# A grouped 1x1 convolution over 512x512 pixels: other runs of rows, other ends of the stores

## The chip, the cores and the metric

The kernel runs on one core of a Trainium2 chip. The metric is the device time of one execution in microseconds (us); the figure for a kernel is the median of its runs. Engines are called by the names that the profile gives them: PE is the matmul engine (PEld its weight loads), DVE the vector engine, ACT the scalar engine, POOL the GpSimd engine and SP the engine that here only issues transfers. SPq, ACTq and POOLq are their sequencers. The core's 16 DMA engines move data between the large memory (HBM) and the on-chip memory (SBUF), whose 128 rows are called partitions.

## The reference, cut to what matters

```python
H = W = 512; G = 4; Cg = 48; C = 192; k = 1
# x: (1, 512, 512, 192) bfloat16, w: (1, 1, 4, 48, 48) bfloat16
xg = x.reshape(1, 512, 512, 4, 48)
out = einsum('bhwgc,gcd->bhwgd', xg, w[0, 0])
return out.reshape(1, 512, 512, 192)
```

For each of 262,144 pixels, four groups of 48 channels are each multiplied by a 48x48 matrix. 100.7 MB are read and as much is written.

## The kernel before

**Columns and fields.** A pixel has 192 values of 2 bytes, 384 bytes. The image is laid out as fields one behind the other. In a full field each of the 128 partitions holds a run of consecutive pixels; its length in pixels is the field's number of columns. A column is thus one pixel in each partition, 49,152 bytes. `plan_fields` (L84) makes, from `FRONT` (L46): a full field of 560 columns, a partial field of 48, full fields of 32 and 880, a partial one of 48, full ones of 32 and 456, which is 2056 columns. In a partial field (`PARTIAL`, L41) only 120 of the 128 partitions hold pixels: all but 16 to 19 and 48 to 51. It moves in five blocks of rows, two of 16 rows through SP and ACT, and three of 44, 12 and 32 rows through POOL. The numbers of a block are its queue, first row, rows, the outer size of its DRAM pattern (4, 4, 11, 3 and 8, so 4 rows of each part belong together), and the columns that it has less. `UNEVEN` (L45) takes 16 columns from the first block of the second partial field, so that the rest of the image divides by 4 x 128 pixels. PE and ACT work on all 128 partitions of such a field; the unused ones are not stored.

**Rings.** The input ring `ring` holds 240 columns, three slots of 80. The output ring `oring` holds 280. `plan_pieces` (L102) cuts fields into loads: 8, 24 and 48 columns first (`HEAD`), then 80 each, and a partial field in one piece. A partial field's 48 columns and the 32 of the full field behind it fill one slot together, a mixed slot. A column's place in the ring is its number modulo 240 (L72 and L256). `plan_stores` (L116) cuts fields into stores at the ring's places 72, 140, 212 and 280 (`OGRID`), at most 40 columns long in the last 240 and with ends at the last 68, 44, 24 and 8 columns (`LAST_PARTS`).

**Engines.** SP (L312) issues the loads in order; each waits until PE has transposed the columns whose place it takes (`freed`, L264). PE works on groups of 4 columns, two groups to a pair: 12 transposes through the identity into PSUM (L350), then, one pair behind, 12 matmuls (L370) with a block matrix that L332 built from the weights. PE waits for a load's semaphore at the first group of a slot; a mixed slot is released by POOL, which waits for all its parts (L299, L300). PE's pairs 9 to 248 run in a loop of 8 rounds of 30 pairs, since a round of 60 groups returns to the same place in the ring. DVE copies the transposes to SBUF (L409). ACT copies each group's result into the output ring (L446) and issues a store once the group after its last has been computed (L427); before it writes to a place it waits for the store that left from there (`landed`, L420). POOL issues its blocks of the partial fields (L296, L307) and, ahead of the blocks of 44 and 12 rows, a small filler transfer (L286).

**Queues.** Loads that SP issues go through queue q1, stores of ACT through q10, POOL's transfers through q0.

Of the kernel before, what the change touches and what calls it, by code (L numbers as in the profile page):

```python
# [1 line left out]

# [22 lines left out]
BIG = 80  # L25
SLOTS = 3
RCOLS = SLOTS * BIG
OGRID = (72, 140, 212, 280)
OCOLS = OGRID[-1]
HEAD = (8, 24, 48)  # L30
LATE_COLS = 240
LATE_PART = 40
LAST_PARTS = (24, 20, 16, 8)
# [5 lines left out]
FULL = (("sync", 0, 128, 128, 0),)  # L39

PARTIAL = (  # L41
    ("sync", 0, 16, 4, 0), ("sync", 32, 16, 4, 0),
    ("pool", 52, 44, 11, 0), ("pool", 20, 12, 3, 0), ("pool", 96, 32, 8, 0),
)
UNEVEN = (("sync", 0, 16, 4, 16), *PARTIAL[1:])  # L45
FRONT = ((6, ((48, PARTIAL), (32, FULL))), (11, ((48, UNEVEN), (32, FULL))))  # L46

FILL_ROWS = 5
FILL_BEFORE = (2, 3)


class Field:


    def __init__(self, cols, blocks, g0, pix):
        self.cols, self.g0, self.g1 = cols, g0, g0 + cols // 4
        self.full = blocks is FULL
        self.blocks = []
        for (queue, r0, rows, outer, less) in blocks:
            self.blocks.append((queue, r0, rows, outer, pix, cols - less))  # L60
            pix += rows * (cols - less)
        self.pix_end = pix
        assert cols % 4 == 0


class Piece:

    def __init__(self, i, field, c0, size):
        self.i, self.field = i, field
        self.c0, self.c1, self.size = c0, c0 + size, size  # L70
        self.g0, self.g1 = field.g0 + self.c0 // 4, field.g0 + self.c1 // 4
        self.at = 4 * self.g0 % RCOLS  # L72
        self.full, self.blocks = field.full, field.blocks
        assert size % 4 == 0 and self.at + size <= RCOLS

# [7 lines left out]

def plan_fields(npix):  # L84

    parts, head = [], sum(HEAD)
    for slots, special in FRONT:
        parts += [(head + BIG * slots, FULL), *special]
        head = 0
    cols = npix - sum((n - b[4]) * b[2] for n, blocks in parts for b in blocks)  # L90
    if cols < 128 * BIG:
        parts, cols = [], npix
    assert cols % 512 == 0
    fields, g, pix = [], 0, 0
    for n, blocks in [*parts, (cols // 128, FULL)]:
        fields.append(Field(n, blocks, g, pix))
        g, pix = fields[-1].g1, fields[-1].pix_end
    assert pix == npix
    return fields


def plan_pieces(fields):  # L102
    pieces = []
    for f in fields:
        first = [f.cols]
        if f.full:
            first = list(HEAD) if not f.g0 and sum(HEAD) <= f.cols else []
        c = 0
        while c < f.cols:
            n = first.pop(0) if first else min(BIG, f.cols - c)  # L110
            pieces.append(Piece(len(pieces), f, c, n))
            c += n
    return pieces


def plan_stores(fields):  # L116
    total = 4 * fields[-1].g1
    stores, at = [], 0
    for f in fields:
        c = 0  # L120
        if not f.full and at + f.cols > OCOLS:
            at = 0
        ends = []
        if f is fields[-1] and f.cols > LATE_COLS:
            ends = [f.cols - sum(LAST_PARTS[i:]) for i in range(len(LAST_PARTS))]
        while c < f.cols:
            if f.full:
                end = min([g for g in OGRID if g > at + 24] or [OCOLS]) - at + c
                if f.cols < BIG:
                    end = min(OCOLS - at + c, f.cols)  # L130
                if ends and c >= f.cols - LATE_COLS:
                    end = min(OCOLS - at, LATE_PART) + c
                end = min([end, f.cols] + [e for e in ends if e > c])
            else:
                end = f.cols
            stores.append(Store(f, c, end, at))
            c, at = end, (at + end - c) % OCOLS
    return stores


class Unit:


    def __init__(self, pieces):
        self.pieces, self.g0, self.g1 = pieces, pieces[0].g0, pieces[-1].g1
        self.slot = pieces[0].at // BIG
        self.regular = pieces[0].at % BIG == 0 and 4 * (self.g1 - self.g0) == BIG


def plan_units(pieces):  # L150
    units, rest = [], list(pieces)
    while rest:
        n = 1
        if rest[0].g0 and rest[0].at % BIG == 0:
            while n < len(rest) and rest[n].at % BIG:
                n += 1
        units.append(Unit(rest[:n]))
        rest = rest[n:]
    return units
# [19 lines left out]
def bass_standalone__grouped__vision_kernel(nc, x, w, out):  # L179
# [3 lines left out]
    assert npix % 512 == 0, "the pixel count must be a multiple of 512"  # L183

    fields = plan_fields(npix)
    pieces = plan_pieces(fields)
    stores = plan_stores(fields)
    units = plan_units(pieces)
    unit_of = {g: u for u in units for g in range(u.g0, u.g1)}
    store_of = {g: s for s in stores for g in range(s.g0, s.g1)}  # L190
# [12 lines left out]
    def transfers(ap, tile, part, queues):  # L203
        f, c0, c1, at = part.field, part.c0, part.c1, part.at
        for n, (queue, r0, rows, outer, pix, cols) in enumerate(f.blocks):
            if queue not in queues:
                continue
            px = ap[pix:pix + rows * cols, :]
            if f.full:
                view = px.rearrange("(p i) n -> p (i n)", p=rows)[:, c0 * C:c1 * C]  # L210
            else:
                assert (c0, c1) == (0, f.cols)
                view = px.rearrange("(c a i) n -> a c (i n)", a=outer, c=rows // outer)
            yield n, view, tile[r0:r0 + rows, at * C:(at + (c1 - c0 if f.full else cols)) * C]
# [12 lines left out]
    with ExitStack() as es:  # L227
# [25 lines left out]
        fill_sem = [sem(f"fill{k}") for k in range(4 * len(mixed))]  # L253

        def columns(g):
            at = 4 * g % RCOLS  # L256
            return ring[:, at * C:(at + 4) * C]

        def out_columns(g):
# [9 lines left out]
        def _(gp):  # L269
# [12 lines left out]
            def filler():  # L282
                k = len(used)
                src = xf[0:2 * FILL_ROWS, 0:4].rearrange("(t p) n -> p t n", t=2)
                dst = fill[:, 8 * k:8 * k + 8].rearrange("p (t n) -> p t n", t=2)
                gp.dma_start(dst, src).then_inc(fill_sem[k], 16)  # L286
                used.append(k)

            for nth, u in enumerate(mixed):
                part = [p for p in u.pieces if not p.full]  # L290
                for p in part:
                    gp.wait_ge(t_done, freed(p))
                    for n, dram, sbuf in transfers(xf, ring, p, ("pool",)):
                        if n in FILL_BEFORE:
                            filler()
# [6 lines left out]
                for i, s in enumerate(stores):  # L302
                    if any(s.field is p.field for p in part):
                        for n, dram, sbuf in transfers(of, oring, s, ("pool",)):
                            if n in FILL_BEFORE:
                                filler()
# [174 lines left out]
```

## Time and profile before

| what | us |
|---|---|
| median of 9 runs | 477.94 (477.2 to 479.64) |
| profiled execution | 477.95 |
| its span, first to last instruction | 476.2 |
| ACT: 514 copies of a group, 801 ns each | 387.4 |
| DVE: 257 copies of a pair, 958 ns each | 246.2 |
| PE busy | 431.5 |
| 22 loads of 3840 KB, median from issue to landing | 27.0 |
| 11 stores of 3456 KB, the same | 41.2 |
| 10 stores of 3264 KB, the same | 41.4 |
| first store issued by ACT at | 26.3 |
| last load issued by SP at | 409.3 |

The span is the profiled execution's time from its first to its last instruction; 1.75 us of its time lie around it. Busy times of different engines overlap, and a transfer's time from issue to landing includes the time that it stands in a queue. The page's two rows in 40 digits, DMA and GB/s, give the state of the DMA engines over the span.

### The profile page before, as it was taken

Reading aid. Unit: us, or ns where it says so; the run is one execution under the profiler, and the core shown is the slowest. Engines: PE = TensorE matmul, PEld = TensorE weight load, DVE = VectorE, ACT = ScalarE, POOL = GpSimd, SP = SyncE. Lnnn points to the kernel's source line nnn. Section 1 sums busy time; section 2 is a strip of 40 time slices with the busy share of each in tenths; the row PEclk is TensorE's granted clock in tenths of the full one; section 3 lists DMA queues with packets and bytes.
Section 4 is the critical chain, followed back from the end, with each engine's and each line's share of the span. In section 5 each row is a group of like instructions: output and inputs, shape, how many; then the busy total and the mean of one; then the engine's idle time right before and its main releaser. Section 6 shows DMA issues by size and latency. Waiting matters only on the chain.

```text
span 476.2 us, 13580 instructions
## 1 busy us (share of the span) xinstructions
PE 431.5 (91%) x6178; PEld 390.3 (82%) x6178; DVE 246.9 (52%) x258; ACT 388.7 (82%) x515; POOL 12.5 (3%) x28
## 2 busy tenths in 40 slices
PE   4999999999698999999997996999978998997993
PEld 4988889888697898888896896898877987886882
DVE  2555555555354555555553553555545555552551
ACT  2898899988587998998895885999868997976884
POOL 1000000200002000000000000200002000000000
PEclk9999999999899999999998997999989999998997
DMA  8999999999999999999999999999999999999997
GB/s 327 434 399 429 431 431 430 423 428 437 437 430 427 431 424 435 436 437 422 427 433 437 437 430 422 435 421 439 431 432 428 432 427 426 424 437 433 422 414 294
DMA packets 10674, 201.57 MB, mean 423 GB/s; under 512 B 2112, under 2 KB 2112, under 8 KB 2752
## 3 DMA queue, kind: packets, MB, share of 16 engines
q1 hardware_dynamic: 4320, 97.44, 48.0%
q10 hardware_dynamic: 5120, 97.42, 47.8%
q0 software_dynamic: 1216, 6.49, 3.3%
q8 instruction: 9, 0.15, 0.1%
q14 instruction: 9, 0.07, 0.0%
HBM read 100.68 MB, written 100.66 MB: 423 GB/s over the span
## 4 chain that ended last, share of the span: by engine, by line
PE 48%; DMA 39%; ACT 8%; issue 1%; ACTq 1%; another core or an unknown queue 1%; SPq 0%; POOLq 0%
DMA out_dram<-oring 30%; PE o_ps L370 28%; PE xT_ps L350 20%; DMA ring<-in_x_dram 9%; ACT oring L446 8%; ACTq L427 1%; SPq L320 0%; SPq L313 0%; ACTq L420 0%; POOLq L300 0%; POOLq L299 0%; ACTq L429 0%
## 5 line engine op out<-in xcount | busy, mean ns | idle before, releaser
L446 ACT CAST oring<-o_ps 128x768 bf16<-128x768 f32 x514 | 387.4, 801 | 80.2 <-PE o_ps L370 55.3
L409 DVE COPY xT_sb<-xT_ps 128x1536 bf16<-128x1536 bf16 x257 | 246.2, 958 | 216.7 <-PE xT_ps L350 216.7
L370 PE MATMUL o_ps<-wt,xT_sb 128*128 128x144 bf16 (+1 forms) x3084 | 290.0, 237 | 27.2 <-ACT oring L446 21.5
L370 PEld LDWEIGHTS o_ps<-wt,xT_sb 128*128 128x128 bf16 x3084 | 213.3, 99 | 65.6 <-ACT oring L446 56.2
L350 PE MATMUL xT_ps<-ident,ring 128*128 128x128 bf16 x3084 | 222.2, 223 | 7.0 <-POOLq L300 3.6
L350 PEld LDWEIGHTS xT_ps<-ident,ring 128*128 128x128 bf16 x3084 | 190.2, 100 | 9.7 <-POOLq L300 3.8
L286 POOL DMA_DIRECT2D fill<-in_x_dram x8 | 4.6, 575 | 350.6 <-PE xT_ps L350 235.8
L296 POOL DMA_DIRECT2D ring<-in_x_dram x6 | 3.4, 562 | 0.0
L307 POOL DMA_DIRECT2D out_dram<-oring x6 | 3.3, 558 | 0.0
L332 PE MATMUL o_ps<-w_sb,esel 48*128 48x48 bf16 x10 | 0.6, 210 | 2.7 <-DMA w_sb<-in_w_dram 2.7
L332 PEld LDWEIGHTS o_ps<-w_sb,esel 48*128 48x128 bf16 x10 | 0.5, 113 | 2.7 <-POOL esel L273 2.7
L402 DVE CAST wt<-o_ps 128x480 bf16<-128x480 f32 x1 | 0.7, 658 | 3.3 <-PE o_ps L332 3.3
L446 ACT ACT_TABLE_LOAD x1 | 1.3, 1283 | 0.8 <-PEq L466 0.8
L273 POOL TENSOR_SCALAR_AFFINE_SELECT esel<-esel 48x272 bf16<-48x272 bf16 x1 | 0.4, 404 | 0.0
L270 POOL MEMSET esel<- 48x272 bf16 x1 | 0.3, 318 | 0.3 <-POOLq L466 0.3
L277 POOL TENSOR_SCALAR_AFFINE_SELECT ident<-ident 128x128 bf16<-128x128 bf16 x1 | 0.3, 284 | 0.0
L271 POOL MEMSET ident<- 128x128 bf16 x1 | 0.2, 198 | 0.0
L466 POOL MEMSET const-float32-0.0<- 128x1 f32 x1 | 0.1, 99 | 0.3 <-issue 0.3
L466 POOL MEMSET const-bfloat16-1.0<- 128x1 bf16 x1 | 0.1, 103 | 0.0
L466 POOL MEMSET const-uint8-127<- 128x1 uint8 x1 | 0.1, 103 | 0.0
L466 POOL MEMSET const-float32-1.0<- 128x1 f32 x1 | 0.1, 99 | 0.0
## 6 DMA issues: line engine op xcount, KB each, us to landing
ring<-in_x_dram SPq DMA_DIRECT2D x22, 3840.0 KB, 27.0
out_dram<-oring ACTq DMA_DIRECT2D x11, 3456.0 KB, 41.2
out_dram<-oring ACTq DMA_DIRECT2D x10, 3264.0 KB, 41.4
out_dram<-oring ACTq DMA_DIRECT2D x3, 1920.0 KB, 19.5
out_dram<-oring ACTq DMA_DIRECT2D x1, 3840.0 KB, 47.4
ring<-in_x_dram SPq DMA_DIRECT2D x2, 1536.0 KB, 31.3
out_dram<-oring ACTq DMA_DIRECT2D x2, 1536.0 KB, 43.3
out_dram<-oring ACTq DMA_DIRECT2D x1, 2880.0 KB, 39.0
```

The lines of the kernel that those rows point to most:

```text
L273: gp.affine_select(out=esel[:], in_=esel[:], pattern=[[-1, ECOLS]], compare_op=AluOpType.is_equal, fill=0.0, base=ESHIFT, channel_multipli ...
L286: gp.dma_start(dst, src).then_inc(fill_sem[k], 16)
L296: gp.dma_start(sbuf, dram).then_inc(ld_sem[ld_key[p.i, n]], 16)
L307: gp.dma_start(dram, sbuf).then_inc(st_sem[i][n], 16)
L332: last = pe.matmul(o_ps[:, NOB - 1, col:col + CG], lhsT=esel[:, s0:s0 + 128], rhs=w_sb[:, g, :], start=True, stop=True, skip_group_check=True)
L350: last = pe.transpose(xT_ps[:, g % NXP, j * 128:(j + 1) * 128], xg[:, j * 128:(j + 1) * 128], ident[:])
L370: last = pe.matmul(o_ps[:, v % NOB, c0_:c1_], lhsT=xs[:, j * 128:(j + 1) * 128], rhs=wt[:, WOFF[tc]:WOFF[tc] + (c1_ - c0_)], start=(tc == ...
L402: dve.tensor_copy(wt[:], o_ps[:, NOB - 1, 0:WCOLS]).then_inc(wc_sem, 1)
L409: dve.tensor_copy(xT_sb[pair % NXS][:, 0:n * 2 * UC].rearrange("p (g c) -> p g c", g=n), xT_ps[:, b0:b0 + n, 0:2 * UC]).then_inc(e_done[pa ...
L427: act.dma_start(dram, sbuf).then_inc(st_sem[i][n], 16)
L446: act.copy(out_columns(g).rearrange("p (u c) -> p u c", u=2), o_ps[:, v % NOB:v % NOB + 2, 0:UC]).then_inc(fa_done[g % (2 * NTOK)] if g < ...
L466: nc = _bacc.Bacc("TRN2", target_bir_lowering=False, num_devices=1)
```

## The change

`OGRID` becomes (92, 188, 280): a store ends at about each third of the output ring instead of each quarter. The first field's stores end after 8, 32 and 92 columns (`FIRST_STORES`). The head is 88 columns (8, 24, 56) instead of 80, and the place of a column in the input ring becomes its number less 88, modulo 240, so that the head ends at the ring's end and the slots begin with column 88. The partial fields have 44 columns, and the first 36 of the full field behind each fill the slot; those 36 are no field of their own any more but the first piece of a run of 916 or 484. `UNEVEN` takes 11 columns from the first block and 12 from the block of 12 rows.

The loads are then 8, 24, 56, 6 of 80, 44, 36, 11 of 80, 44, 36, 5 of 80 and 48. The stores are 8, 24, 60, 96, 92, 92, 96, 92 and 8 columns, the partial 44, then 40, 96, 92, 92, 96, 92, 92, 96, 92, 92 and 36, the partial 44, and 108, 92, 96, 40, 40, 12, 28, 24, 20, 16 and 8. PE's loop covers pairs 10 to 249.

```diff
-OGRID = (72, 140, 212, 280)
+OGRID = (92, 188, 280)
-HEAD = (8, 24, 48)
+HEAD = (8, 24, 56)
+FIRST_STORES = (8, 24, 60)
-UNEVEN = (("sync", 0, 16, 4, 16), *PARTIAL[1:])
-FRONT = ((6, ((48, PARTIAL), (32, FULL))), (11, ((48, UNEVEN), (32, FULL))))
+UNEVEN = (("sync", 0, 16, 4, 11), *PARTIAL[1:3], ("pool", 20, 12, 3, 12), PARTIAL[4])
+FRONT = ((6, 44, PARTIAL), (11, 44, UNEVEN))
+def ring_at(g):
+    return (4 * g - sum(HEAD)) % RCOLS
...
-        self.at = 4 * self.g0 % RCOLS
+        self.at = ring_at(self.g0)
...
-    parts, head = [], sum(HEAD)
-    for slots, special in FRONT:
-        parts += [(head + BIG * slots, FULL), *special]
-        head = 0
+    parts, lead = [], sum(HEAD)
+    for slots, cols, blocks in FRONT:
+        parts += [(lead + BIG * slots, FULL), (cols, blocks)]
+        lead = BIG - cols
...
-            n = first.pop(0) if first else min(BIG, f.cols - c)
+            n = first.pop(0) if first else min(BIG - ring_at(f.g0 + c // 4) % BIG, f.cols - c)
...
-        ends = []
+        ends = list(accumulate(FIRST_STORES)) if not f.g0 else []
...
-                if ends and c >= f.cols - LATE_COLS:
+                if f is fields[-1] and c >= f.cols - LATE_COLS:
...
-        self.regular = pieces[0].at % BIG == 0 and 4 * (self.g1 - self.g0) == BIG
+        self.regular = self.g0 > 0 and pieces[0].at % BIG == 0 and 4 * (self.g1 - self.g0) == BIG
...
-        if rest[0].g0 and rest[0].at % BIG == 0:
+        if 4 * rest[0].g0 >= sum(HEAD) and rest[0].at % BIG == 0:
...
-            at = 4 * g % RCOLS
+            at = ring_at(g)
```

## The prediction

> **What bounds the kernel now.** I read the page's list of busy times first, then its DMA queues, then the waits, and last the timeline around two places: where compute stops for a load, and the end.
>
> ```profile
> span 476.2 us, 13580 instructions
> PE 431.5 (91%) x6178; PEld 390.3 (82%) x6178; DVE 246.9 (52%) x258; ACT 388.7 (82%) x515; POOL 12.5 (3%) x28
> ...
> DMA  8999999999999999999999999999999999999997
> ...
> q1 hardware_dynamic: 4320, 97.44, 48.0%
> q10 hardware_dynamic: 5120, 97.42, 47.8%
> q0 software_dynamic: 1216, 6.49, 3.3%
> ```
>
> The 16 DMA engines are busy from the second slice to the last but one, and the three queues of data add up to 99.1% of their span. PE at 91% is no bound: ACT's copies go at one per 0.828 us where nothing stops them (column 80 at 27.46 us, column 160 at 44.33), so 514 of them need 425 us. The bytes are the floor: 201.57 MB at the plateau of 432 GB/s (the trace's packets of 30,720 bytes take 1,138 ns on each of 16 engines) is 466.6 us.
>
> ```profile
> DVE xT_sb L409 <- PE xT_ps L350: 216.7, 257, 6.3
> ...
> ACT oring L446 <- PE o_ps L370: 55.3, 135, 8.3
> ...
> ACT oring L446 <- DMA out_dram<-oring: 18.2, 8, 4.7
> ...
> PE xT_ps L350 <- POOLq L300: 3.6, 1, 3.6
> PE xT_ps L350 <- DMA ring<-in_x_dram: 3.4, 2, 1.9
> ```
>
> So compute waits for the DMA almost only on the store side: ACT stops 8 times until an old store has left the output ring. PE waits for a load once after the head, in the first mixed slot (pieces of 48 and 32 columns), and ACT then stands 4.75 us:
>
> ```profile
> 130.28 1.60 ACT L446 CAST oring<-o_ps 128x768 bf16<-128x768 f32 x2 [4.75 <-PE o_ps L370]
> ...
> 431.06 1.50 ACT L446 CAST oring<-o_ps 128x768 bf16<-128x768 f32 x2 [4.71 <-DMA out_dram<-oring]
> ...
> 469.73 0.50 ACTq L427 DMA_DIRECT2D out_dram<-oring  x1
> ```
>
> The last stop ends at 431.06; from there ACT makes 44 copies in 38.6 us without a stop, issues the last store at 469.73, and the trace has that store's engines landing between 472.56 and 475.72. Both chains thus end together, and neither has much to spare.
>
> **What the skill says.** "DMA: Bandwidth & Descriptors", section "Queues, rings and completion order": each DMA engine takes the queues that have work in turn, a packet at a time. The DMA view between 200 and 250 us agrees:
>
> ```profile
> q1 hardware_dynamic: 418, 11.37, 52.7%
> q10 hardware_dynamic: 422, 10.15, 47.3%
> ```
>
> As many packets of loads as of stores, and so bytes in the ratio of their sizes (80 columns against 68 or 72). The same page, "The descriptor swizzle", puts rows 16 to 19 and 48 to 51 of a 128-row transfer on one engine, the fifth; these are the rows that the 120-row pieces leave out. The trace agrees: after the first such piece one engine lands its part of the stores 7.2 us before the middle one, and loses 3.7% of time from there (lead 7.2 us at 194, 3.4 at 300). And "Where 436 GB/s comes from" gives a ceiling of 435 GB/s, beside 432 measured: no size of packet can bring more than 0.7%.
>
> **The change, part by part.** I count in columns: 128 rows of 384 bytes, 0.1138 us at 432 GB/s. There are 2056 to load and 2056 to store, in both kernels (560+48+32+880+48+32+456 and 568+44+916+44+484), 467.9 us of DMA. By the packet records the sum of columns moved at time t is (t - c) / 0.1138 with c = 4.2 us at 84, 4.7 at 264 and 5.6 at 444.
>
> *Number of transfers.* Loads stay 30 pieces; stores fall from 37 to 33. A packet of 3,072 bytes takes 121 ns and one of 30,720 takes 1,138, so each has about 8 ns of its own; 4 stores of 8 rows per engine less is 32 x 8 ns = 0.26 us gained. Issues on ACT (0.34 us) and SP lie beside DMA work: 0.
>
> *Head and first stores.* The first store is issued near 13 us, not 26.34. The loads fill the DMA until then, so nothing is gained: 0. Where the stores begin now, the DMA share falls to 0.51 between 30 and 31 us, about 1 us lost over the dip; whether smaller first stores shrink it no row shows: -0.9 to 0, I take 0. The third piece lands some 0.9 us later (8 columns more), before its first transpose at 14.78 us: 0. The ring now starts at column 152, so the second 80-column piece waits for the first pair of transposes (6.2 us) with 88+80 columns, 19 us of DMA, queued: 0.
>
> *Thirds.* Store packets become 35,328 or 36,864 bytes beside loads of 30,720, so the turn about now favours stores by 53.5 to 46.5, where it favoured loads by 53 to 47. The store queue drains as fast as ACT fills it, and ACT's 18.2 us of waits for stores go. What is late next are the loads: they lose 0.74 columns per us against ACT (4.09 against 4.83).
>
> *Mixed slots.* On the first four engines a 44-column piece takes 8 packets and the 36-column piece behind it another 8, each in turn with a store packet of 1.31 to 1.36 us. PE waits for the last of them. The sum of columns gives its time. For the kernel before, with 640 loaded and 437 stored on those engines, 1077 x 0.1138 + 4.5 + 0.8 for the landing = 127.9, and the trace has 127.85. After, at most 648 loaded and 560 stored (more isn't issued yet): 137.4 + 5.3 = 142.8, so ACT resumes column 568 at 145.2 (2.4 us later, as before) instead of 128.8: idle 16.4 us, not 4.75. In the second slot at most 1608 + 1492: 352.7 + 6.0 = 358.8, and column 1528 is copied at 361.2 (before: near 347, though column 1600 at 366.6 after ACT's own waits). POOL issues the same 20 transfers; its last load of each slot landed at 124.56 and 336.63 before, 38 and 33 us after its issue, and is not the last to land now: 0. The bound from below is the kernel before: a wait of 4 us; I take the upper one, since the stores are ready in time.
>
> *Does the DMA run dry behind these waits?* Just ahead of the next load's issue at column 728, 888 columns of loads and 652 of stores are out, 1540, and 1520 are moved: 2.3 us in hand. At column 1688: 3420 against 3412, 0.9 us. Nothing is lost, barely.
>
> *End.* From 361.2, 352 columns at 0.2069 us bring ACT to column 1880 at 434.0; the same 38.6 us as before end it at 472.6, against 469.7; the fastest landing seen after the last issue was 2.8 us, so 475.5 at the latest from this chain. The DMA chain: 88 columns of stores are still queued when ACT reaches 1990, so the starved windows of the end (0.92, 0.91 and 0.88 between 460 and 470, 0.6 us) fill: -0.6. One engine also fetched instructions for 0.96 us at 468.9 and was the last by 1.06 us; that may fall elsewhere: 0 to -1, I take 0.
>
> *Four columns less left out.* The fifth engine gets 2 x 4 x 8 rows x 384 bytes x 2 ways = 49 KB more, 1.8 us; it led the middle by 5 us near 460. Engines 8 to 15 carry the same: 0.
>
> Sum: -0.26 - 0.6 = -0.9 us on a profiled run of 477.95 (span 476.2 and 1.75 around it), which is the median of the runs, 477.94, too: 477.0, and I write 476.9.
>
> **Rivals.**
> *The queue runs dry (slower).* One mechanism: if PE resumes column 1528 later than about 362 us, the DMA has nothing left before the loads and the 108-column store that column 1688 sets free, and ACT's end moves with it; each us later costs a us. The margin of 0.9 us is less than the 2 to 3 us by which landings spread over engines. For it: 16 us of PE wait replace 5, and lead is never regained. Against it: the bound assumes every issued store done. At 3 to 4 us over: 480.3.
> *The end gets clean (faster).* The dip at the first stores goes (-0.9) and the fetch falls off the last engine (-1) beside the -0.9: 475.2 to 476.2. For it: both are seen once, at a place that the change moves; against it: nothing ties either to store size.
> *The left-out rows were the point.* The fifth engine idles in the thin stretches, loses its lead and, slower by 3.7%, ends last: about +1, 478.9. Against: 5 us of lead, less 1.8.
> *The change doesn't act:* if stores still back up, ACT waits at column 1852 for the 108-column store, 7 copies earlier than now at 1880, and ends 5.8 us later: 481. The packet sizes speak against it.
>
> **How the numbers follow.** A difference of 0.2%, about 1 us, is what a measurement here can tell. Forecast 0.40 (476.2 to 477.8: 0.20 faster, 0.18 within, 0.02 slower), clean end 0.25, dry queue 0.25, fifth engine 0.05, stores backed up 0.05. Faster 0.20 + 0.25 = 0.45; within 0.18; slower 0.02 + 0.25 + 0.05 + 0.05 = 0.37. The range runs from the clean end, 475.2, to the dry queue, 480.3.
>
> **What would show it.** ACT's wait for stores near 0; PE's waits for the mixed slots of 14 to 17 us each, near 126 to 143 and 344 to 359; packets one to one with q10 ahead in bytes; DMA share above 0.95 through 177 and 393 us; ACT's last copy near 472. A DMA share well under 0.9 behind a wait makes the dry queue right; ACT waiting at 1852 makes my whole order of loads and stores wrong.

## The result and the profile after

| | before | after |
|---|---|---|
| median of the runs, us | 477.99 (477.2 to 480.07, 31 runs) | 486.51 (479.8 to 503.71, 10 runs) |
| profiled execution, us | 477.95 | 485.07 |
| its span, us | 476.2 | 483.2 |
| last store issued by ACT at | 469.73 | 476.14 |
| last engine of the last store lands at | 475.72 | 482.74 |

The ratio is 1.013, with a 95% interval of 1.0105 to 1.0155: slower by about 1%, where the prediction had 476.9 us, a little faster. Run again later beside other kernels, the same code gave 1.0083 (1.0051 to 1.0115). The ratios compare the undisturbed runs alone, so they stand below that of the two medians above. The changed kernel also scatters more from run to run than the kernel before.

The page of the changed kernel, the lines that answer to those shown in the prediction:

```profile
span 483.2 us, 13572 instructions
PE 433.6 (90%) x6178; PEld 391.4 (81%) x6178; DVE 246.9 (51%) x258; ACT 388.2 (80%) x515; POOL 12.5 (3%) x28
...
DMA  8999999999999999999999999999999999999984
...
q1 hardware_dynamic: 4320, 97.77, 47.6%
q10 hardware_dynamic: 4544, 97.75, 47.6%
q0 software_dynamic: 1216, 5.84, 2.9%
```

The engines' busy times are as before, the same 201.57 MB are moved, and the row of the DMA looks as full as before. Nothing on this page says where 7 us went. The waits do (engine, line, releaser: us in total, times, longest):

```profile
ACT oring L454 <- PE o_ps L378: 68.8, 127, 8.0
PEld o_ps L378 <- ACT oring L454: 46.0, 148, 5.1
PE xT_ps L358 <- DMA ring<-in_x_dram: 21.1, 7, 5.5
...
ACT oring L454 <- DMA out_dram<-oring: 4.9, 1, 4.9
```

ACT's waits for stores went from 18.2 us to 4.9, as the change to larger stores would do, and PE's waits for loads came in their place: 21.1 us instead of 3.4. Some 3 us of this line are two waits in the head, which every kernel here has; a mixed slot, which POOL releases, stands in a line of its own (3.6 us before, 0.9 after). The timeline of ACT shows where (start, length, what, and in brackets the idle time before it and its releaser):

```profile
116.67 1.60 ACT L454 CAST oring<-o_ps 128x768 bf16<-128x768 f32 x2 [6.35 <-PE o_ps L378]
119.55 4.77 ACT L454 CAST oring<-o_ps 128x768 bf16<-128x768 f32 x6 [1.28 <-PE o_ps L378]
...
135.30 0.80 ACT L454 CAST oring<-o_ps 128x768 bf16<-128x768 f32 x1 [1.18 <-PE o_ps L378]
135.71 0.34 ACTq L435 DMA_DIRECT2D out_dram<-oring  x1
...
337.84 1.60 ACT L454 CAST oring<-o_ps 128x768 bf16<-128x768 f32 x2 [5.91 <-PE o_ps L378]
...
446.40 1.60 ACT L454 CAST oring<-o_ps 128x768 bf16<-128x768 f32 x2 [5.51 <-PE o_ps L378]
...
476.14 0.34 ACTq L435 DMA_DIRECT2D out_dram<-oring  x1
```

116.67 us is column 480, 337.84 is 1440 and 446.40 is 1920; a shorter stop of 3.1 us stands at 1280. Each lies 8 columns ahead of a full slot whose load came late, since PE transposes a pair of groups before it multiplies the pair ahead of it (the load for the slot at 1928 landed at 444.06). None is a mixed slot: ahead of the first of these, which begins at column 568, ACT stops 1.18 us, at 135.30, and not 16.4. The store issued at 135.71 is column 468 to 560, and it is the line to remember: of the stores ahead of it, fifteen of the sixteen engines had landed their parts by then (the last one at 135.99).

The DMA view of 200 to 250 us, packets and MB by queue:

```profile
q10 hardware_dynamic: 374, 11.78, 54.7%
q1 hardware_dynamic: 362, 9.92, 46.0%
```

Packets one to one, and bytes now in favour of stores. And one line that wasn't looked at before, the window from 84 to 460 us (length, busy us of PE, PEld, DVE, ACT and POOL, granted clock, DMA share, GB/s), of the kernel before:

```profile
84.00:460.00 376.00, 346.97 (x4979) 314.39 (x4980) 198.65 (x208) 312.41 (x415) 11.00 (x20) 0.97 1.00 430
```

and of the changed kernel:

```profile
84.00:460.00 376.00, 343.10 (x4891) 310.61 (x4889) 194.62 (x205) 306.37 (x408) 11.22 (x20) 0.96 1.00 427
```

The DMA is "busy" for all of both windows, share 1.00, and moves 427 instead of 430 GB/s: over 376 us that is 376 x 3 / 430, about 2.6 us. The lost time hides in longer packets, not in gaps. Counted from the packets, as c in the prediction (the time less 0.1138 us for each column moved, recounted for both kernels in the same way):

| at, us | 84 | 120 | 140 | 264 | 400 | 440 | 460 |
|---|---|---|---|---|---|---|---|
| c before | 4.55 | 4.68 | 4.68 | 4.87 | 5.46 | 5.60 | 5.78 |
| c after | 4.24 | 4.57 | 6.12 | 6.29 | 6.98 | 8.14 | 8.33 |

The last landing moved by 7.0 us. 2.6 us of it are lost by 460 (8.33 less 5.78). Another 3.1 are lost from there until the middle engine lands the last store (479.04 instead of 473.4, which is 5.6 later): ACT is late with the last columns, so stores come in thin. The last 1.4 are one engine that lands 3.7 us after the middle one, where it was 2.3.

### The profile page after: what moved, and what is told of

It reads as the page before. It is cut to its first block, busy times and chain, and to the rows that moved or that the text cites. A ratio compares the mean times of both kernels' runs of the same rounds, so it can differ in the third digit from the quotient of the medians.

```text
span 483.2 us, 13572 instructions
## 1 busy us (share of the span) xinstructions
PE 433.6 (90%) x6178; PEld 391.4 (81%) x6178; DVE 246.9 (51%) x258; ACT 388.2 (80%) x515; POOL 12.5 (3%) x28
## 2 busy tenths in 40 slices
DMA packets 10098, 201.57 MB, mean 417 GB/s; under 512 B 2048, under 2 KB 2048, under 8 KB 2944
## 4 chain that ended last, share of the span: by engine, by line
PE 45%; DMA 43%; ACT 7%; ACTq 1%; issue 1%; SPq 0%; POOLq 0%
DMA ring<-in_x_dram 34%; PE o_ps L378 26%; PE xT_ps L358 20%; DMA out_dram<-oring 9%; ACT oring L454 7%; ACTq L435 1%; SPq L328 0%; SPq L321 0%; POOLq L308 0%; POOLq L307 0%; ACTq L437 0%; ACTq L428 0%
## 5 line engine op out<-in xcount | busy, mean ns | idle before, releaser
L358 PE MATMUL xT_ps<-ident,ring 128*128 128x128 bf16 x3084 | 222.8, 223 | 22.0 <-DMA ring<-in_x_dram 21.1
## 6 DMA issues: line engine op xcount, KB each, us to landing
ring<-in_x_dram SPq DMA_DIRECT2D x22, 3840.0 KB, 33.7
```

The source lines that it names most:

```text
L358: last = pe.transpose(xT_ps[:, g % NXP, j * 128:(j + 1) * 128], xg[:, j * 128:(j + 1) * 128], ident[:])
```

## The experiments

The table holds them all; "packet" is the length of most store packets in columns, a load packet being 80 unless noted. GB/s is that of the window 84 to 460 us. Waits and GB/s are those of one profiled execution each. For "96s halved" (489.19 us) and "thirds, no partial fields" (501.35 us) it was longer than the median, so their waits are too high; for "later thin end" (480.08 us) it was among the shortest.

| what | ends of stores | packet | ratio to before | PE waits for loads, us | ACT waits for stores, us | GB/s |
|---|---|---|---|---|---|---|
| before | quarters | 68, 72 | 1 | 3.4 | 18.2 | 430 |
| after | thirds | 92, 96 | 1.013 (1.0105 to 1.0155) | 21.1 | 4.9 | 427 |
| after, again | thirds | 92, 96 | 1.0083 (1.0051 to 1.0115) | 22.2 | 4.8 | 426 |
| rest of the change, quarters | quarters | 68, 72 | 0.9995 (0.9975 to 1.0016) | 2.9 | 18.6 | 430 |
| before, only thirds | thirds | 92, 96 | 1.0255 (1.019 to 1.0321) | 26.3 | 1.2 | 423 |
| after, all stores halved | thirds | 46, 48 | 1.0205 (1.0159 to 1.0251) | 2.9 | 21.9 | 425 |
| after, sixths | sixths | 44 to 48 | 1.0121 (1.0086 to 1.0157) | 3.2 | 21.0 | 426 |
| after, fifths | fifths | 56 | 1.0071 (1.0045 to 1.0097) | 3.0 | 24.3 | 427 |
| before, ring of 208 | thirds of 208 | 68, 72 | 1.0158 (1.0111 to 1.0205) | 3.1 | 30.9 | 428 |
| before, loads halved | quarters | 68, 72 (loads 40) | 1.0218 (1.0179 to 1.0257) | 37.1 | none | 419 |
| after, 96s halved | thirds | 92, 48 | 1.0107 (1.0083 to 1.0132) | 3.0 | 23.1 | 424 |
| halves, stores halved | halves | 70 | 1.0226 (1.0186 to 1.0266) | 3.0 | 23.7 | 420 |
| quarters, stores halved | quarters | 34, 36 | 1.0201 (1.0155 to 1.0247) | 3.0 | 6.9 | 425 |
| after, later thin end | thirds | 92, 96 | 1.0093 (1.0059 to 1.0128) | 16.3 | 2.9 | 428 |
| thirds, no partial fields | thirds | 92, 96 | 1.0367 (1.0323 to 1.0411) | 43.3 | none | 412 |
| quarters, no partial fields | quarters | 68, 72 | 1.025 (1.023 to 1.027) | 5.4 | 31.1 | 429 |

### Which part of the change

The changed kernel with the ends of the stores put back, and all else of the change kept:

```diff
-OGRID = (92, 188, 280)
+OGRID = (72, 140, 212, 280)
-FIRST_STORES = (8, 24, 60)
+FIRST_STORES = (8, 24, 40)
```

> The changed kernel with the stores' ends back at quarters of the output ring (72, 140, 212, 280; first stores 8, 24, 40), all else as changed. Theory A (store packets larger than the load packets of 30,720 bytes take more than half of each turn, so loads fall behind and PE waits for them): with 26,112 and 27,648 bytes the loads lead again, PE's waits for loads fall from 21 us to under 8, ACT's waits for stores rise towards 18, last copy on ACT before 472, time 478 to 480. Theory B (the 44-column pieces leave less of the fifth engine's rows out, so that one engine is late): the size of the stores doesn't matter, time stays at 484 to 487 and one engine still lands 3 us or more after the others.

Measured: 478.25 us, 0.9995. Its waits:

```profile
ACT oring L454 <- DMA out_dram<-oring: 18.6, 10, 5.1
...
PE xT_ps L358 <- DMA ring<-in_x_dram: 2.9, 2, 1.6
```

The kernel before, with thirds alone:

```diff
-OGRID = (72, 140, 212, 280)
+OGRID = (92, 188, 280)
```

> The kernel before with one line changed: the stores end at thirds (92, 188, 280). Theory A: PE now waits for loads (15 us or more in all), time 483 to 487. Theory B: the 48-column pieces still leave the rows out as before, time 477 to 479. Theory C (head, first stores and the shifted ring matter): also 477 to 479.

Measured: 490.52 us, 1.0255, above the 483 to 487 that I had expected, with the same exchange of waits. So the thirds carry the whole loss. Head, run lengths, 44-column pieces and their left-out rows together are worth nothing that can be measured; with thirds they even soften it (1.013 or 1.0083 against 1.0255), by what, no run here tells.

### Too large a packet, or too coarse an end

A store end at thirds changes two things at once: packets grow from 26 to 28 KB to 35 to 37 KB beside loads of 30.7 KB, and the ring comes free, and stores are issued, in three parts instead of four. First, the packets: every full store of 80 columns or more leaves as two half-column transfers at the same moment, still waited for together.

```diff
+            def halved(s):
+                return s.field.full and s.c1 - s.c0 >= 80
...
-                        act.wait_ge(one, 16)
+                        act.wait_ge(one, 32 if halved(stores[i]) else 16)
...
-                    act.dma_start(dram, sbuf).then_inc(st_sem[i][n], 16)
+                    cut = (s.c1 - s.c0) // 2 * C if halved(s) else 0
+                    if cut:
+                        act.dma_start(dram[:, :cut], sbuf[:, :cut]).then_inc(st_sem[i][n], 16)
+                    act.dma_start(dram[:, cut:], sbuf[:, cut:]).then_inc(st_sem[i][n], 16)
```

> The changed kernel with each full store of 80 columns or more issued as two transfers of half the columns, both at the moment of the one before: packets of 17,664 or 18,432 bytes, while the ends in the ring and the moments of issue stay at thirds. Theory A (size of a packet in the turn): loads get 63% of the turns' bytes, PE's waits for loads fall under 8 us, ACT waits for stores instead, time 478 to 482. Theory A2 (thirds are too coarse for the ring: the store queue runs empty and then fills too late, whatever the packets): PE's waits stay near 20 us and the time at 484 to 487.

Measured: 487.19 us, 1.0205. The load waits are gone, and nothing is gained: ACT now stops at the output ring, at columns 748 and 1680 for 8.3 and 9.2 us. That the load waits follow the packets' lengths is shown; that they are the loss isn't, since the time is above both ranges that I had written.

The other direction, on the kernel before with its stores untouched: each load of 80 columns as two of 40 at the same moment.

```diff
...
-                    sp.dma_start(sbuf, dram).then_inc(ld_sem[ld_key[p.i, n]], 16)
+                    cut = p.size // 2 * C if ld_key[p.i, n][0] == "slot" else 0
+                    if cut:
+                        sp.dma_start(sbuf[:, :cut], dram[:, :cut]).then_inc(ld_sem[ld_key[p.i, n]], 16)
+                    sp.dma_start(sbuf[:, cut:], dram[:, cut:]).then_inc(ld_sem[ld_key[p.i, n]], 16)
...
```

The waits for these loads count both halves.

> The kernel before with each load of 80 columns issued as two of 40 at the same moment, freed and waited for together: load packets of 15,360 bytes beside store packets of 26,112 and 27,648, so that stores take 64% of each turn's bytes; ring and stores as before, in quarters. Theory A (share of the turn): PE waits for loads 15 us or more, the store queue runs dry between stores, time 481 to 487. Theory D (depth of the ring alone): no more waits than before, 477 to 479.

Measured: 489.08 us, 1.0218, above the 481 to 487 that I had expected. Its wait line, and its window:

```profile
PE xT_ps L353 <- DMA ring<-in_x_dram: 37.1, 13, 13.3
```

```profile
84.00:460.00 376.00, 337.49 (x4884) 304.83 (x4882) 194.32 (x203) 305.79 (x407) 11.17 (x20) 0.97 1.00 419
```

With quarters and the same stores, load packets shorter than store packets are enough to bring the load waits and the loss: this is the picture of the changed kernel, doubled. Share 1.00 again, at 419 GB/s.

Finer ends with small packets, at sixths and at fifths of the ring:

```diff
-OGRID = (92, 188, 280)
+OGRID = (48, 92, 140, 188, 236, 280)
```

> The changed kernel with stores ending at sixths of the output ring (48, 92, 140, 188, 236, 280): packets of 16,896 to 18,432 bytes, as the halved thirds had (17,664 and 18,432), but each store issued when its own columns are done and landing by itself. Theory D (three parts in the ring are too few: one being written, and a store that lands only as a whole): 477 to 480, ACT's waits for stores under 15 us. Theory P (small store packets give the loads 63% of the bytes and the stores come too late, whatever the ring's parts): about as the halved thirds, 485 to 489, ACT's waits over 18 us.

```diff
-OGRID = (92, 188, 280)
+OGRID = (56, 112, 168, 224, 280)
-FIRST_STORES = (8, 24, 60)
+FIRST_STORES = (8, 24, 24)
```

> The changed kernel with stores at fifths of the ring (56, 112, 168, 224, 280; first stores 8, 24, 24). Theory D: more parts give more slack, 476.5 to 478.5, no store issued into an empty queue after the first. Theory P: loads lead more, ACT waits for stores 20 us or more, 479 to 483.

Measured: 483.57 us, 1.0121, which lies between the two theories' ranges, and 481.6 us, 1.0071, in that of theory P. The load waits are gone here too and ACT stops at the ring for 21.0 and 24.3 us. Sixths have the packets of the halved thirds, and are 3.6 us faster than these in the medians: the ends seem to count beside the packets, though these two ran on different chips.

Less ring with the packets of before: the output ring of the kernel before cut to 208 columns.

```diff
-OGRID = (72, 140, 212, 280)
+OGRID = (72, 140, 208)
```

> The kernel before with an output ring of 208 columns in three parts (72, 140, 208) in place of 280 in four: packets stay at 26,112 and 27,648 bytes, smaller than the loads'. Theory D: three parts are too few, ACT's waits for stores rise from 18 us to 35 or more, time 484 to 492. Theory A (only the size of the packets beside the loads' counts): loads still lead, PE never waits for them, time 478 to 481.

Measured: 485.35 us, 1.0158; ACT waits 30.9 us for stores, under the 35 that I had expected. At equal packets a shorter ring costs time; whether by its columns or by having three parts instead of four, this run can't tell.

Then the two properties apart. Only the 96-column stores of the changed kernel are halved, so that a round of the ring has packets of 92, 48, 48 and 92, 70 in the mean as with quarters, and ends at thirds. Against the halved kernel:

```diff
-                return s.field.full and s.c1 - s.c0 >= 80
+                return s.field.full and s.c1 - s.c0 == 96
```

> The changed kernel, but each full store of 96 columns leaves as two half-column transfers of 48 columns at the same moment; stores of 92 stay whole. Store packets are then 92, 48, 48 and 92 columns long in each round of the output ring, 70 in the mean as with quarters, while the stores still end at thirds. If the balance of packet lengths between the two queues is all that matters: PE's waits for loads fall from 21 us to under 5, ACT's waits for stores come near the 18 us of the kernel before, none much above 5 us, and the time is within 0.3% of the kernel before, about 477 to 479. If coarse ends cost something of their own (a third of the ring comes free at once, and with halves for every store the ring stopped ACT for 8 to 9 us): one or two ACT stops of 6 to 9 us remain and the time lies between, 480 to 484. If packet length has nothing to do with it: as the changed kernel, 484 to 487, with PE's load waits unchanged.

Measured: 483.26 us, 1.0107, in the same session as the changed kernel again with 1.0083. The theory that the balance of packet lengths is all falls. The waits of its one profile:

```profile
ACT oring L460 <- DMA out_dram<-oring: 23.1, 5, 7.9
...
PE xT_ps L358 <- DMA ring<-in_x_dram: 3.0, 2, 1.6
```

The loads of full slots are in time (PE waits 3.6 us for the first mixed slot), and in exchange ACT stops five times at the ring, up to 7.9 us. Then ends at halves with packets of 70 columns, and ends at quarters with packets of 34 to 36, both from the halved kernel:

```diff
-OGRID = (92, 188, 280)
+OGRID = (140, 280)
-FIRST_STORES = (8, 24, 60)
+FIRST_STORES = (8, 24, 40, 68)
```

> The changed kernel with store ends at the halves of the output ring (140 and 280), first stores of 8, 24, 40 and 68 columns, and each full store of 80 columns or more issued as two transfers of half its columns at the same moment. Store packets are then 70 columns long as with quarters; only the ends are twice as coarse. If coarse ends cost by themselves (places come free and stores are issued 140 columns at a time): PE's load waits stay under 5 us, ACT's waits for the ring rise well above the 18.6 us of quarters, with stops of 8 us or more, the time is above 484 and the cost grows from thirds to halves. If the packets' lengths alone decide: as quarters, 477 to 479.5, ACT's waits near 18 us.

```diff
-OGRID = (92, 188, 280)
+OGRID = (72, 140, 212, 280)
-FIRST_STORES = (8, 24, 60)
+FIRST_STORES = (8, 24, 40)
...
-                return s.field.full and s.c1 - s.c0 >= 80
+                return s.field.full and s.c1 - s.c0 >= 64
```

> The changed kernel with store ends at quarters (72, 140, 212, 280; first stores 8, 24, 40), and each full store of 64 columns or more issued as two transfers of half its columns at the same moment. Ends are those of quarters; store packets are 34 to 36 columns beside loads of 80. If packet lengths shift the turns: loads lead further, stores back up, ACT's waits for the ring rise from 18.6 to 25 us or more, PE's load waits stay under 4 us, and the time is 480 to 484. If only the coarseness of the ends decides: as quarters, 477 to 479.5.

Measured: 490.46 us, 1.0226, and 486.52 us, 1.0201. Halves, whose packets are those of quarters:

```profile
ACT oring L460 <- DMA out_dram<-oring: 23.7, 7, 7.7
...
PE xT_ps L358 <- DMA ring<-in_x_dram: 3.0, 2, 1.7
```

```profile
84.00:460.00 376.00, 338.75 (x4851) 306.38 (x4849) 193.46 (x203) 304.15 (x405) 11.17 (x20) 0.96 1.00 420
```

Quarters, whose packets are half as long:

```profile
ACT oring L460 <- issue: 16.1, 15, 3.7
ACT oring L460 <- DMA out_dram<-oring: 6.9, 2, 3.5
...
PE xT_ps L358 <- DMA ring<-in_x_dram: 3.0, 2, 1.7
```

Coarse ends at the right packets cost 2.3%, and short packets at the right ends cost 2.0%. A small part of the second is the number of packets: two of 13,056 bytes take 8 ns more than one of 26,112 (2 x 488 against 968), and each engine has 198 more of them, 1.6 us in all. In the first the longest stop is 7.7 us, a little under the 8 that I had written, and another 10.5 us of ACT's idle time have no releaser. In the second most of ACT's stops stand under "issue", time with no releaser in the profile, so the wait line for stores alone (6.9) would mislead. The two lines sum to 23.0 us, under the 25 that I had written and hardly more than with whole quarters (18.6 and 4.3). The time is above the 480 to 484 that I had written: what costs here are longer packets, c growing by 5.9 us (next section).

This kernel also shows where "one to one" ends. Its window of 200 to 250 us:

```profile
q10 hardware_dynamic: 819, 9.88, 46.9%
q1 hardware_dynamic: 418, 11.37, 53.4%
```

Two store packets to one of the loads, and the bytes divide as with whole stores (10.14 to 11.43 MB in the same window). Where the packets are joined end to start into engines, load and store packets go in turn while both are queued; then the loads run out, and eight or so store packets go alone. Over a longer stretch the rings make both sides move the same; the packets' lengths decide how long a transfer takes (loads land in 19.0 us here, in 24.4 beside whole stores).

### What is lost when a queue runs empty

Each of these kernels loses DMA time in packets that grow longer while the share stays near 1.00. In the changed kernel it can be watched at 135.71, the store issued after nearly all others had landed: its first packet on any engine starts at 139.70, 4.0 us later, and between 136.8 and 139.7, 22 of 30 load packets of 30,720 bytes, which take 1,138 ns otherwise, take 1.33 to 2.03 us. c grows by 0.66 us from 120 to 130, while one store is left on its way, and by 0.89 from 130 to 140. The very first store of the kernel before shows the same (issued 26.34, first packet 30.57, 0.9 us lost between 28 and 32).

I counted, from the issues and the landings on each engine, how often a store met a store queue that was empty on an engine up to 466 us, and how many loads issued between 84 and 420 us met a thin load queue (fewer than 16 engine shares of earlier loads still on their way, less than one load):

| kernel | stores into an empty queue (engines x stores) | loads into a thin queue | c from 84 to 460, us |
|---|---|---|---|
| before | 20 | 3 | 1.2 |
| rest of the change, quarters | 16 | 3 | 1.5 |
| after | 55 | 3 | 4.1 |
| halves, stores halved | 282 (both halves of a store counted) | 12 | 10.2 |
| quarters, stores halved | 17 | 16 | 5.9 |

16 of each first column is the first store, which cannot be avoided. Where loads are late, the stores run out; where loads lead, they run out themselves, because ACT at the full ring stops PE and no slot comes free. Quarters are the one case among these in which neither queue empties. So from kernel to kernel the count goes with the loss.

Inside the changed kernel the count explains little. The store issued at 350.80 found the store queue empty on all 16 engines, too; its first packets came 3.65 to 4.94 us later on fifteen of them (1.53 on one), but only three load packets grew beyond 1.25 us, and c rose by 0.16 us from 350 to 360. Loads alone are not slow either: from 134.0 to 136.8, with hardly a store on its way, all 40 took 1,138 to 1,140 ns. And from 400 to 440, where c grows by 1.16 us, no store was issued into an empty queue and no load into a thin one; there load packets of up to 2.17 us stand between 417 and 420, where one store's last packets give way to the next one's. The stores that met an empty queue on most engines (135.71, 350.80 and 391.27) thus account for little more than 1 us of the 4.1 that c grows; what lengthens the other packets stays open.

### Does it come through the four engines of the 16-row blocks?

The time from issue to landing is that of the last engine. Split by engine it looks different. Landings in us after issue, sorted, for a load near 228 us and a store near 178 us:

```
before, load  issued 230.15: 24.0 24.5 24.6 24.6 24.7 24.7 25.5 25.6 25.7 25.7 25.9 25.9 26.0 26.2 27.0 27.7
after,  load  issued 225.36: 22.2 22.2 22.4 22.4 22.5 24.4 24.5 26.6 27.2 27.5 28.5 28.8 28.9 29.0 29.3 31.5
before, store issued 178.95: 33.2 38.5 38.9 39.5 39.6 39.7 39.7 39.7 40.0 40.5 40.6 40.7 40.8 40.9 40.9 41.2
after,  store issued 177.14: 25.0 30.1 30.4 30.6 30.6 30.7 30.8 30.9 31.0 31.2 31.3 31.6 39.8 39.9 41.2 42.1
```

From the first partial field on, four engines land each store 8 to 11 us after the other twelve, later 5 to 9, until 315 us; the loads spread in turn. Four engines are as many as carry the 16-row blocks of the partial fields. To tell cause from company, both ends without any partial field (one full field of 2048 columns):

```diff
-FRONT = ((6, 44, PARTIAL), (11, 44, UNEVEN))
+FRONT = ()
```

> The changed kernel (ends at thirds) without partial fields: the image is one full field of 2048 columns, all 128 rows, so no block of 16 rows and no POOL transfer; the full result is computed. To be read beside the next kernel, the same with ends at quarters, since the fifth DMA engine, 3.7% slower, now gets no relief in either. If the loss of thirds comes through the four DMA engines that carry the 16-row blocks and then stay 8 to 11 us out of step: without the blocks no group of four is late, PE's load waits fall well under 20 us, and thirds come within 0.5% of quarters here. If it comes from the packets' turns and the coarse ends alone: PE's load waits stay at 20 us or more, and thirds are 1% or more above quarters, as with the partial fields.

> The same without partial fields, with ends at quarters (72, 140, 212, 280). In both theories PE's load waits stay under 5 us and ACT waits for the ring; the slow fifth engine sets the end, so I expect 480 to 490 us. It serves as the measure for the thirds beside it: the difference between the two is near 0 if the four late engines carry the loss, 5 us or more if turns and coarse ends do.

Measured: thirds 1.0367 (1.0323 to 1.0411), quarters 1.025 (1.023 to 1.027); the ratios differ by 1.2%, about as much as with the partial fields. Thirds:

```profile
PE xT_ps L358 <- DMA ring<-in_x_dram: 43.3, 14, 5.3
```

Quarters:

```profile
ACT oring L454 <- DMA out_dram<-oring: 31.1, 11, 4.0
...
PE xT_ps L358 <- DMA ring<-in_x_dram: 5.4, 4, 2.4
```

PE's load waits with quarters are a little above the 5 us that I had written. There is no group of four, and thirds cost about what they cost before, so thirds need no group of four to cost time. But the pair doesn't settle what the group does in the changed kernel, since one slow engine takes its place here: of the load issued at 266.79, fifteen engines land after 11.5 to 20.2 us and the last after 40.2. The rest of the change with quarters is the better witness. It has the same 16-row blocks, and of its load issued at 201.40 all engines land after 22.0 to 23.6 us, of its store issued at 195.61 fifteen after 36.6 to 41.0 and one, ahead, after 30.3. So the blocks alone put no four engines behind.

The spread over the engines is most of the changed kernel's load waits all the same. After the head, PE waits for four loads:

| PE begins to wait at, us | middle engine lands at | last engine lands at |
|---|---|---|
| 108.88 | 111.95 | 114.32 |
| 293.50 | 291.62 | 296.09 |
| 330.88 | 331.17 | 335.50 |
| 439.59 | 433.68 | 444.06 |

Only at the first was the middle engine late by more than 0.3 us. At the last, fifteen engines had landed by 438.65, and PE waited 4.5 us for one. What spreads the engines in this way was not tried.

### The end

The stop at column 1920 (446.40) lies inside the last 240 columns, where stores shrink to 40 columns. The shorter stores were begun 240 columns earlier:

```diff
-LATE_COLS = 240
+LATE_COLS = 480
```

> The changed kernel with stores of at most 40 columns from the last field's first store on (480 columns before the end, not 240). Theory A: in the last field packets of 15,360 bytes let the loads go ahead, the stop of 5.5 us at column 1920 goes, ACT's last copy comes near 471 instead of 476, time 479 to 482. If the end is set by one late engine whatever the loads do (Theory B), the last landing stays 3 us behind the others and the time above 483.

Measured: 483.22 us, 1.0093 (1.0059 to 1.0128). In the profile the stop at 1920 is gone, another of 4.75 us stands at 1360, and PE's load waits are 16.3 us (with 2.7 more for a mixed slot), but the interval overlaps both of those of the changed kernel. It settles nothing about the time.

> The changed kernel once more, for a second profile of it. If one DMA engine's late end (its last store packet came 3 us after the other engines') belongs to the kernel, the last landing is again some 3 us behind the middle one; if it was an accident of that execution, the spread of the last store's landings is 1 to 2 us. In both cases PE's waits for loads stay at 18 to 24 us, ACT stops on columns 480, 1440 and 1920 return at the same columns, and the time is 485 to 487.

Measured: 482.19 us, 1.0083, below the 485 to 487 that I had expected; the profiled execution took 485.36. The stops return at columns 480, 1280, 1440 and 1920 (3.6, 4.4, 6.9 and 3.8 us), and one engine again lands the last store 3.8 us after the middle one (483.05, middle 479.24). So the late engine belongs to the kernel, at least in its executions of this length. It is late well before the end: in the first profile one engine lands 5.2 to 5.4 us after the next to last in every load from the one issued at 388.67 on, in the second 4.6 in every store from 430 to 467, and in the profile of the later thin end no engine is more than 0.5 us behind there. Which engine it is the landings don't tell, and it wasn't tried.

No kernel tried is faster than the kernel before. The nearest, the rest of the change with quarters, can't be told from it.

## Why the prediction was wrong

**Right.** The turn about, word by word: "Store packets become 35,328 or 36,864 bytes ... so the turn about now favours stores by 53.5 to 46.5". The trace has 374 packets to 362, and 11.78 to 9.92 MB, 54 to 46. That each DMA engine serves its queues in turn by packets is what the Trainium skill says ("DMA: Bandwidth & Descriptors", section "Queues, rings and completion order"), and the trace has the packets (one partition's run each) in turn while both queues have work; the halved loads and halved stores show what follows from it: the length of one queue's packets decides the other queue's waits. That ACT's waits for stores go (18.2 to 4.9 us) and that "what is late next are the loads" was right too. Of the head: c at 84 us is 0.3 us less than before. That is not the 0.26 of fewer packets, since by then no fewer stores have been issued; it is a smaller loss at the first stores, which the prediction named and took at 0. With quarters even this is too small to be measured.

**The step that failed** is the one under "Does the DMA run dry behind these waits?": "Nothing is lost, barely." It summed the columns of both queues and asked when the sum would run out. It never did: the DMA share behind both mixed slots was above 0.95, just as I had written down as the sign that I was right. But a busy DMA lost time, and that was priced at nothing: 1.55 us between 120 and 140 (0 before), where the stores ran low and one began anew, 1.16 us between 400 and 440 (0.14 before), where no queue was found empty. In all it was 2.6 us more than before by 460, and 3.1 us more in the thin end after that. The prediction had seen one such loss, about 1 us at the first store of the kernel before, and did not ask whether it could come again.

**The step before it**, "Mixed slots", failed too: it put the load waits in the wrong place. It took the sum of columns at the mixed slot with 560 stored columns issued, "more isn't issued yet", as a bound, and got 142.8 us. But ACT had stood still at column 480 for 6.35 us, so the store of columns 468 to 560 wasn't issued until 135.71, and the slot landed at 133.79: its own sum with 468 stored columns, (648 + 468) x 0.1138 + 5.3, gives 132.3. The first mixed slot cost PE 0.9 us and the second nothing; the waits, 17.3 us in all, lay in four full slots ahead of and behind them, to which the prediction had given none.

Much of this could have been had from the profile. PE needs a slot again 160 columns after it has emptied it, and at ACT's 0.2069 us a column that is 33.1 us. Loads landed in 27.0 us before; the change takes their share from 53 to 46 of 100, and 27.0 x 53 / 46 = 31.1 us leaves 2 us for the spread over engines. Measured: 33.7. For the middle engine the estimate is right (25.0 before, 28.8 after, and 25.0 x 53 / 46 = 28.8); the rest is the spread, which grew from 2 us to 5. In the same way a place in the output ring is needed (280 - 72) x 0.2069 = 43.0 us after its store of 72 columns was issued, and (280 - 96) x 0.2069 = 38.1 us after one of 96; stores of before landed in 41.2 to 41.4. The thirds thus gave up 5 us of room on the side of the stores, and the 6 us of room that the loads had (33.1 less 27.0) were used up. I had written that loads "lose 0.74 columns per us", and didn't compare what was lost with what the ring holds.

**Its readings.** The pace of 0.207 us a column holds (between columns 160 and 480, 80 columns take 16.5 to 16.6 us), but the two places named for it, columns 80 and 160, give 0.211. The share of 0.51 between 30 and 31 us is not idle DMA either: a window counts a packet where it starts, and the shares of the two windows ahead of it are 1.45 and 1.22. The loss of about 1 us is right. None of this changes the forecast by more than 1.4 us.

**The end.** Predicted were ACT's last copy at 472.6 and the last landing by 475.5; they were at 476.1 and 482.74. ACT was 6.4 us later than before, and its last stop, 5.5 us at column 1920, stands there: the starved windows at the end that should have filled, -0.6, grew instead.

**The rivals.** "The queue runs dry" had the sign, by luck: it meant that the DMA would stand idle behind column 1528, at 480.3 us. ACT copied column 1528 at 357.7, ahead of its limit of 362. It is not what happened. "The left-out rows were the point" doesn't explain the loss, since the rest of the change is neutral with quarters; whether the engine that ends late with thirds is the fifth isn't known. "The clean end" didn't come, and that stores still back up is refuted by the waits.

**What stays open.** The shares of coarse ends and of large packets in the 1%: each alone, carried to a factor of two, costs about 2%, and mending the packets of thirds gains nothing because the ring then stops ACT. What lengthens most of the packets, what spreads the engines, and what sets one engine 3.8 us behind at the end.

## What to carry to other kernels

Where loads and stores share the DMA engines and both have work queued, their packets went in turn here, so longer packets on one side made the other side's transfers land later: compare the landing time of each side with what its ring allows (ring less one transfer, times the pace of compute) before and after, and expect waits where it comes within the spread over engines, for it is the last engine that is waited for. Larger transfers were not free here even at the right packet length, since they are issued and come free in coarser steps; four parts of the ring beat two, three, five and six, of which five and six also had shorter packets. And a DMA share of 1.00 is not full speed: read the GB/s of the window beside it (430, 427 and 419 here at the same share), since lost time can show as longer packets and not as idle time.

## What the hardware showed that I had not expected

- A store issued into an empty store queue while loads flowed started about 4 us later (135.71 to 139.70, 26.34 to 30.57, and 3.65 us or more on fifteen engines at 350.80). Where hardly a load was on its way, it took 0.84 to 0.99 us on fifteen engines (halves, issued at 302.01). Load packets of 1,138 ns grew to as much as 2.03 us in the first of these cases and to 2.10 in the second, and hardly in the third.
- Around a stop of some 6 us PE was granted a lower clock (0.74 and 0.54, where the kernel before has 1.00 in both windows), and ACT has a second gap of 1.28 us a few columns on (119.55 above). The windows of the changed kernel around column 480:

```profile
110.00:116.00 6.00, 1.63 (x15) 1.63 (x16) 0.13 (x1) 0.32 (x1) 0.00 (x0) 0.74 0.98 413
116.00:120.00 4.00, 4.00 (x37) 3.95 (x36) 1.78 (x2) 2.05 (x3) 0.00 (x0) 0.54 1.01 428
```

- One engine was late in the queue that waited longer. Without partial fields one engine trails: with thirds in the loads (issued at 266.79: fifteen engines after 11.5 to 20.2 us, the last after 40.2), with quarters in the stores (issued at 276.83: 29.6 to 35.3, the last after 51.9).
